# A block kernel's attention: the P-times-V bank's store in five parts, SyncE's issues in written order, stores two or three slots later

## The chip, the cores and the metric

The kernel runs on one core of one Trainium2 chip. The metric is the device time of one execution in microseconds (us); lower is better. The core has five engines that run on their own and meet through semaphores: TensorE (PE, with its weight loads shown apart as PEld), VectorE (DVE), ScalarE (ACT), GpSimd (POOL) and SyncE (SP). SP does no arithmetic here: it issues nearly all transfers between HBM and the on-chip memories. Each engine, SP too, takes its instructions strictly in the order in which the program gives them to it, and one that must wait holds up all behind it.

## The reference

A transformer block with both branches in parallel, for 2048 tokens of width 640:

```
xn  = layernorm(x)
q, k, v = split(xn @ wqkv)                       # 32 heads of 20
p   = softmax(mask(q k^T / sqrt(20)))            # a token sees itself and the 255 before it
out = x + (p v) @ wo + (gelu(xn @ w_gate) * (xn @ w_up)) @ w_down    # 1728 hidden columns
```

## The kernel before

The products in float32 are made of a high and a low part each, and three matmuls stand for one. Tokens are worked in four chunks `c` of 512, heads in eight groups `g` of four. Roughly, the program has four stages: layer norm, transposes and the first projections (to 60 to 100 us, mixed with the next); the attention, to 545 us; the gate and up products, to 804 us; and the last products with `w_down` and `wo`.

**The attention** (`attention()`, L816) is a software pipeline written out by hand. It has 32 units `u`, one for each pair of a head group and a chunk, and each unit has 14 slots (`NS`). In a slot the program first does what was put off to it (`defer(n, fn)`, L219, puts `fn` off by `n` slots; `tick()`, L807, gives out what has fallen due), then writes pieces of the attention, then fills the slot with matmuls of other work (`pull_fill`): the projections of later heads, then gate and up products. What a unit does on its slots:

- Slots 0, 5 and 9: `max_pair` (L488), score matmuls in bf16 on PE into `ps_m` (L507), and their row maxima on DVE (L517). These belong to units ahead: the pairs in slot 5 of unit u are the first of unit u+2.
- Slots 1, 3, ... 11: `exp_piece` (L558), score matmuls into `ps_e` (L572), exponentials on ACT into `P` (L574); POOL clears what the mask excludes (`clear`, L587 and L590).
- Slot 0: `av_unit(u - 1)` (L593), the P-times-V matmuls into two banks `ps_o` (L615). ACT copies both out (`ob` at L621, `oc` at L622), POOL joins them into `ob` three slots later (L625), and `store` writes `ob` to HBM five slots later (L628). `ob` has one buffer, [128, 512]: each of the four heads takes 32 of its rows, of which 20 are the output, one is the sum of the exponentials and eleven are not used.
- Slots 9 and 12: `load_stack(u + 3, ...)` (L473), the keys (slot 9) and the queries (slot 12) of unit u+3 from HBM, in six parts each (L482). There are three buffers of queries and four of keys.

**What the filler leaves to store.** A projection of queries or keys (`save_qk`, L248) is split into three bf16 parts in a tile `pt` with two buffers: ACT writes the first (`upper`, L277), DVE and ACT the second, POOL the third (`lowest`, L259), and `store` (L262) sends them to HBM in two or three transfers (L268), one slot after `lowest`. A hidden tile `he` is stored one slot after its product (L689). `x_sums` (L740) makes sums of the activations on POOL for the next stage and stores each `tx` two slots after it is made (L755). Weight tiles `wr` are loaded by `load_qk` (L232) and `load_gu` (L633).

**What sets the order on each queue.** A block `tc.manual_schedule(engines=...)` keeps the instructions of the engines it names in the order in which the program writes them. The attention's block (L871) names PE, ACT and DVE (`MANUAL`) and POOL. SP (`MANUAL_OUT`) is not among them, so the order of its issues in the attention comes from the planner of the framework, which also moves loads ahead of their place in the text. The gate-and-up stage and the last stage have blocks of their own that name SP as well.

**Where the results go.** `od[c]` is one HBM tensor per chunk, [1024, 512]: 32 rows (20 outputs, the sum, eleven unused) of each of 32 heads, row d of head h at d * 32 + h. `sd[c]` is the slice of it with the sums, which a later stage reads (L1085).

Of the kernel before, what the change touches and what calls it, by code (L numbers as in the profile page):

```python
# [9 lines left out]
F32 = mybir.dt.float32  # L10
# [7 lines left out]
S, D, H, DH = 2048, 640, 32, 20  # L18
DF = 1728
C = 512  # L20
NC = S // C
# [27 lines left out]
MANUAL_OUT = {mybir.EngineType.SP}  # L49
MANUAL = {mybir.EngineType.PE, mybir.EngineType.Activation, mybir.EngineType.DVE}  # L50
# [17 lines left out]
def block_kernel(ctx, tc, x, wqk, wv, wgu, wdo, wdl, out):  # L68
    nc = tc.nc

    const = ctx.enter_context(tc.tile_pool(name="const", bufs=1))
    dram = ctx.enter_context(tc.tile_pool(name="dram", bufs=1, space=DRAM))
# [13 lines left out]

    qd = [dram.tile([NG, 3, 4 * DH, C], BF, name=f"qd{c}") for c in range(NC)]
    kd = [dram.tile([NG, 3, 4 * DH, C], BF, name=f"kd{c}") for c in range(NC)]
    od = [dram.tile([32 * H, C], F32, name=f"od{c}") for c in range(NC)]
    sd = [t[D:D + H] for t in od]  # L90
    td = [{i: dram.tile([128, 2, C], F32, name=f"td{p}{i}") for i in (1, 2, 3, 4)} for p in range(NC // 2)]
    wtd = [dram.tile([128, 4, HD], F32, name=f"wtd{q}") if q not in OWN else None for q in range(NQD)]
    rd = [dram.tile([H, C], F32, name=f"rd{c}") for c in range(NC)]
# [1 line left out]
    hd = [hdp[f // 2][:, f % 2] for f in range(NF - 1)] + [dram.tile([NC, 64, C], F32, name="hde")]  # L95
# [102 lines left out]
    now = [None]  # L198
# [20 lines left out]
    def defer(n, fn, *a):  # L219
        if now[0] is None:  # L220
            fn(*a)
        else:
            at(now[0] + n, fn, *a)
# [24 lines left out]
    def save_qk(t, c, ps):  # L248
        pt = qkp.tile([128, 3, C], BF, name="pt", tag="pt")
        r = qkp.tile([128, C], F32, name="r", tag="r", bufs=1)  # L250
        dst = (qd if t < 5 else kd)[c]
        h, l = (2, 0) if t < 5 else (0, 2)

        def lower():
            nc.scalar.activation(pt[:, 1, :], r, AF.Copy)  # L255
            behind(lowest)

        def lowest():
            nc.gpsimd.tensor_tensor(out=pt[:, l, :], in0=r, in1=pt[:, 1, :], op=OP.subtract)  # L259
            defer(1, store)  # L260

        def store():  # L262
            a, end = t % 5 * 128, t % 5 * 128 + 128
            while a < end:
                g, b = divmod(a, 4 * DH)
                n = min(4 * DH - b, end - a)
                p = n - end + a + 128
                nc.sync.dma_start(dst[g, :, b:b + n, :].rearrange("p m t -> m p t"), pt[p - n:p])  # L268
                a += n
            done.add((t, c))  # L270

        def middle():
            nc.vector.tensor_tensor(out=r, in0=ps, in1=pt[:, h, :], op=OP.subtract)
            defer(lag(), lower)

        def upper():
            nc.scalar.activation(pt[:, h, :], ps, AF.Copy)  # L277
            late(middle)

        defer(1, upper)  # L280
# [312 lines left out]
    def av_unit(u):  # L593
        g, c = divmod(u, NC)
        v = vtiles[g]
        os = [psx.tile([128, C], F32, name="ps_o", tag="ex") for _ in range(2)]
        place = {kb - 4 * c: (pts[u, bi], col, q0) for bi, bank in enumerate(pieces(c)) for kb, col, q0, n in bank}

        def half(d, r):
            i = 2 * d + r  # L600
            return d, r, max(0, 64 * i), min(C, 64 * i + 320)

        steps_ = [((0, 0), (0, 1)), ((2, 0), (-1, 1)), ((-1, 0), (2, 1)), ((1, 0), (1, 1)),
                  ((3, 0), (-2, 1)), ((-2, 0), (3, 1))]
        todo = [half(*x) for pair in steps_ for x in pair if x[0] in place]
        begun_, left = set(), [sum(t[1] == r for t in todo) for r in range(2)]
        for d, r, qa, qb in todo:
            pt, col, q0 = place[d]
            kb = 4 * c + d
            assert (id(v), kb) in done, (u, kb)  # L610
            left[r] -= 1
            rows = slice(64 * r, 64 * r + 64)
            for j in range(4):
                w0_ = kb * 84 + 21 * j
                nc.tensor.matmul(os[r][32 * j:32 * j + 32, qa:qb], v[rows, w0_:w0_ + 32],  # L615
                                 pt[rows, j, col + qa - q0:col + qb - q0], start=r not in begun_,
                                 stop=not left[r], skip_group_check=True, tile_position=(64 * r, 32 * j))
            begun_.add(r)
        ob, oc = ap.tile([128, C], F32, name="ob", tag="ob", bufs=1), pts[u, 2][:, 0]
        lo = 0 if c else 64  # L620
        nc.scalar.activation(ob, os[0], AF.Copy)  # L621
        nc.scalar.activation(oc[:, lo:], os[1][:, lo:], AF.Copy)  # L622

        def join():
            nc.gpsimd.tensor_tensor(out=ob[:, lo:], in0=ob[:, lo:], in1=oc[:, lo:], op=OP.add)  # L625

        def store():
            nc.sync.dma_start(od[c].rearrange("(d h) t -> h d t", h=H)[4 * g:4 * g + 4], ob)  # L628

        defer(3, join)  # L630
        defer(5, store)

    def load_gu(f):  # L633
        raws = []
# [24 lines left out]
    def gate_up_fill(f, ws, c):  # L659
        cs = slice(c * C, (c + 1) * C)  # L660
        pss = []
        st = {}

        def c1():
            gs = st["g"] = hp.tile([128, C], F32, name="gs", tag="gs")
            t = st["t"] = hp.tile([128, C], F32, name="he", tag="he", bufs=2)
            nc.scalar.activation(gs, pss[0], AF.Copy, scale=0.5)
            nc.scalar.activation(t, pss[0], AF.Square, scale=math.sqrt(0.044715))
            defer(1, late, c2)

        def c2():
            gs, t = st["g"], st["t"]
            nc.vector.scalar_tensor_tensor(t, t, 1.0, gs, op0=OP.add, op1=OP.mult)
            defer(lag(), c3)

        def c3():
            nc.scalar.activation(st["t"], st["t"], AF.Tanh, scale=2.0 * math.sqrt(2.0 / math.pi))
            st["tanh"] = now[0]

        def c4():  # L680
            nc.vector.tensor_tensor(out=st["g"], in0=pss[1], in1=st["g"], op=OP.mult)
            defer(1, late, c5)

        def c5():
            if now[0] is not None and st.get("tanh", now[0]) >= now[0]:
                defer(1, late, c5)
                return
            nc.vector.scalar_tensor_tensor(st["t"], st["t"], 1.0, st["g"], op0=OP.add, op1=OP.mult)
            defer(1, lambda: nc.sync.dma_start(hd[f][c], st["t"]))  # L689

        for i, (wh, wl) in enumerate(ws):
            ps = psd.tile([128, C], F32, name="ps_d", tag="dn")
            pss.append(ps)
            yield from dense_steps(ps, lambda k: wh[:, k, :], lambda k: wl[:, k, :],
                                   lambda k: xh[:, k, cs], lambda k: xl[:, k, cs], KT)
            defer(1, *((late, c4) if i else (c1,)))
# [43 lines left out]
    def x_sums(p, k, half):  # L740
        w = C // 2
        a, b = (slice((2 * p + i) * C + half * w, (2 * p + i) * C + half * w + w) for i in (0, 1))
        eh, el = xh.bitcast(F32), xl.bitcast(F32)
        live = {}

        def tile_of(i):
            live[i] = ap.tile([128, w], F32, name="tx", tag="tx")
            return live[i]

        def pool(o, i, j, op):  # L750
            nc.gpsimd.tensor_tensor(out=o, in0=i, in1=j, op=op)  # L751

        def store(i):
            t = live[i]
            defer(2, lambda: nc.sync.dma_start(td[p][i][:, k, half * w:half * w + w], t))  # L755

        def s1():
            pool(tile_of(1), eh[:, k, b], eh[:, k, a], OP.subtract)

        def s2():  # L760
            pool(live[1], live[1], el[:, k, b], OP.add)

        def s3():
            pool(live[1], live[1], el[:, k, a], OP.subtract)
            store(1)

        def s4():
            pool(tile_of(2), eh[:, k + 2, b], live[1], OP.subtract)

        def s5():  # L770
            pool(live[2], live[2], el[:, k + 2, b], OP.add)
            store(2)

        def s6():
            pool(tile_of(4), eh[:, k + 2, a], live[2], OP.subtract)

        def s7():
            pool(live[4], live[4], el[:, k + 2, a], OP.add)
            store(4)

        def s8():
            pool(tile_of(3), eh[:, k + 2, b], eh[:, k, b], OP.subtract)

        def s9():
            pool(live[3], live[3], el[:, k + 2, b], OP.add)

        def s10():
            pool(live[3], live[3], el[:, k, b], OP.subtract)
            store(3)

        return s1, s2, s3, s4, s5, s6, s7, s8, s9, s10
# [76 lines left out]
        run(fill)  # L868
        assert not acts

    with tc.manual_schedule(engines=MANUAL | {mybir.EngineType.Pool}):  # L871
        attention()
    pr.close()
    pp.close()
# [454 lines left out]
    w = tiles, sums  # L1329
# [28 lines left out]
    for j, f in enumerate(range(NFA, NF - 1)):  # L1358
# [50 lines left out]
        if not end:  # L1409
            w = nxt_w[0], sums  # L1410
# [115 lines left out]
```

## Time and profile before

| | us |
|---|---|
| median of 3 runs (lowest, highest) | 1047.0 (1046.81, 1047.27) |
| the profiled execution's own time | 1046.35 |
| its span, first to last instruction | 1044.6 |
| PE busy / DVE / ACT / POOL | 1034.0 / 741.1 / 527.6 / 385.9 |

TensorE's granted clock is 1.00 throughout. The 16 DMA engines moved 161.60 MB, at a mean of 155 GB/s.

How to read the rows below. Times are us from the start of the span. A row of the timeline has start, duration, engine and line, operation, what is written from what is read, and how many instructions it merges; in brackets, how long the engine was idle before it and what released it. "SPq" is SP's queue issuing a transfer: the duration there is the issue alone, not the transfer. A row of the waits has who waited for whom, then total, times and longest. A row of the chain of waits has start and length of one piece of the chain that ended last; a "DMA" piece lasts from the issue until the transfer has landed. A row of the stages has the window, its length, and the busy time of PE, PEld, DVE, ACT and POOL with the number of instructions, then the clock, the share of the DMA engines' time and GB/s. Ends of matmuls are modelled, so a busy PE is not a PE at its peak.

### The profile page before, as it was taken

The page shows a single profiled execution, that of the slowest core. Times are in us where ns is not written, and L with a number is a line of the kernel's source. Part 1 is how long each engine was busy: PE and PEld are TensorE (multiplying, and loading weights), DVE is VectorE, ACT ScalarE, POOL GpSimd, SP SyncE. Part 2 cuts the span into 40 slices and gives each one's busy share as a digit, 9 for nine tenths or more (in the row PEclk, how much of TensorE's full clock was granted, in tenths as well). Part 3 has the DMA queues.
Part 4 walks back from the last instruction along what each step waited for, and adds up shares of the span by engine and source line. Part 5 has one row for each costly group of instructions (what it writes and reads, how often), then busy time and mean ns, then how long its engine had stood idle before and what let it go on. Part 6 is the DMA issues. An engine that isn't in the chain of part 4 may idle for free.

```text
span 1044.6 us, 25328 instructions
## 1 busy us (share of the span) xinstructions
PE 1034.0 (99%) x9393; PEld 834.9 (80%) x9393; DVE 741.1 (71%) x2018; ACT 527.6 (51%) x1120; POOL 385.9 (37%) x623
## 2 busy tenths in 40 slices
PE   9999999999999999999999999999999999999998
PEld 8887666666787666666678888888888999999998
DVE  7755666676656576777736788775556888888887
ACT  4534767667666666666676232223224554433332
POOL 5122778888666787667470111101110000000000
PEclk9999999999999999999999999999999999999999
DMA  5552356655533464434225575663217874433333
GB/s 211 179 162 78 115 169 175 183 170 163 160 105 107 131 177 145 139 106 154 64 85 197 177 251 206 253 244 111 78 56 254 267 248 137 137 126 121 119 121 106
DMA packets 102276, 161.60 MB, mean 155 GB/s; under 512 B 12892, under 2 KB 53980, under 8 KB 102152
## 3 DMA queue, kind: packets, MB, share of 16 engines
q1 hardware_dynamic: 99768, 153.82, 45.9%
q10 hardware_dynamic: 2384, 6.16, 1.7%
q8 instruction: 74, 1.21, 0.5%
q14 instruction: 50, 0.41, 0.1%
HBM read 101.78 MB, written 57.80 MB: 153 GB/s over the span
## 4 chain that ended last, share of the span: by engine, by line
PE 89%; DVE 4%; POOL 2%; DMA 2%; issue 1%; ACT 1%; SPq 0%; DVEq 0%; POOLq 0%; ACTq 0%
PE ps_g L970 23%; PE ps L1242 23%; PE ps_d L108 18%; PE ps_e L572 7%; PE ps_v L108 7%; PE ps_o L615 5%; PE ps_m L507 4%; DVE junk L517 2%; PE ps_g L108 1%; DMA od<-ob 1%; PE ps_d L356 1%; POOL tx L751 0%; PE ps_t L185 0%; DMA qs<-qd 0%; ACT P L574 0%
## 5 line engine op out<-in xcount | busy, mean ns | idle before, releaser
L517 DVE CUSTOM_DVE_ANT_0 junk<-ps_m,mask 128x320 bf16<-128x320 f32 (+2 forms) x512 | 242.5, 474 | 130.5 <-PE ps_m L507 72.7
L574 ACT ACTIVATE P<-ps_e 128x512 f32<-128x512 f32 (+2 forms) x384 | 198.6, 571 | 68.5 <-PE ps_e L572 67.8
L1242 PE MATMUL ps<-wb,at 128*128 128x320 f32 x999 | 155.9, 309 | 0.0
L1242 PEld LDWEIGHTS ps<-wb,at 128*128 128x128 f32 x999 | 148.9, 188 | 0.2
L587 POOL TENSOR_SCALAR_AFFINE_SELECT P<-P 128x256 f32<-128x256 f32 (+1 forms) x192 | 95.2, 498 | 72.5 <-ACT P L574 69.0
L572 PE MATMUL ps_e<-qs,ks 124*128 124x128 bf16 (+2 forms) x704 | 118.6, 278 | 0.5 <-ACT P L574 0.3
L108 PE MATMUL ps_d<-xh,wqh 128*128 128x512 f32 x310 | 99.0, 422 | 0.2 <-ACT xh L193 0.2
L108 PE MATMUL ps_d<-xl,wqh 128*128 128x512 f32 x310 | 98.5, 421 | 0.0
L108 PE MATMUL ps_d<-xh,wql 128*128 128x512 f32 x310 | 97.6, 418 | 0.0
L101 POOL TENSOR_TENSOR wql<-wr,wqh 128x640 fp32r<-128x640 f32 x12 | 19.2, 1607 | 195.4 <-PE ps_g L970 150.8
L572 PEld LDWEIGHTS <-ks 124*128 124x128 bf16 x704 | 49.5, 98 | 49.8 <-issue 35.6
L1242 PE MATMUL ps<-wt,at 128*128 128x320 f32 x552 | 88.9, 309 | 0.0
L1242 PEld LDWEIGHTS ps<-wt,at 128*128 128x128 f32 x552 | 82.9, 188 | 0.1
L590 POOL TENSOR_SCALAR_AFFINE_SELECT P<-P 128x512 f32<-128x512 f32 (+1 forms) x144 | 76.9, 542 | 16.3 <-ACT P L574 16.3
L1196 ACT ACTIVATE at<-ss 128x512 fp32r<-128x512 f32 x59 | 37.2, 631 | 82.4 <-DVE ss L1075 82.4
L615 PE MATMUL ps_o<-P,v 64*32 64x320 f32 (+4 forms) x2816 | 74.2, 347 | 0.0
L259 POOL TENSOR_TENSOR pt<-r,pt 128x512 bf16<-128x512 f32 x40 | 46.8, 1171 | 67.4 <-ACT pt L255 67.4
L507 PE MATMUL ps_m<-ks,qs 60*64 60x320 bf16 (+3 forms) x1472 | 65.4, 260 | 4.0 <-DVE mx L517 1.5
L615 PEld LDWEIGHTS ps_o<-P,v 64*32 64x32 f32 x2816 | 50.8, 106 | 21.5 <-issue 0.9
L507 PEld LDWEIGHTS <-qs 60*64 60x64 bf16 x1472 | 29.5, 105 | 44.5 <-issue 37.7
L108 PEld LDWEIGHTS ps_d<-xh,wqh 128*128 128x128 f32 x310 | 56.0, 189 | 10.5 <-issue 1.6
L108 PEld LDWEIGHTS ps_d<-xh,wql 128*128 128x128 f32 x310 | 56.0, 189 | 10.2 <-issue 1.1
(195 smaller groups left out, 1966.6 us busy)
## 6 DMA issues: line engine op xcount, KB each, us to landing
hd<-he SPq DMA_DIRECT2D x50, 256.0 KB
hr<-hd SPq DMA_DIRECT2D x48, 256.0 KB
wr<-wgu SPq DMA_DIRECT2D x27, 320.0 KB
od<-ob SPq DMA_DIRECT2D x32, 256.0 KB
qs<-qd SPq DMA_DIRECT2D x64, 120.0 KB
ks<-kd SPq DMA_DIRECT2D x64, 120.0 KB
xi<-x SPq DMA_DIRECT2D x16, 320.0 KB
qs<-qd SPq DMA_DIRECT2D x64, 80.0 KB
```

Source lines behind the costliest of these rows:

```text
L108: nc.tensor.matmul(ps, a(k), b(k), start=n == 0, stop=n == 3 * nk - 1)
L259: nc.gpsimd.tensor_tensor(out=pt[:, l, :], in0=r, in1=pt[:, 1, :], op=OP.subtract)
L507: nc.tensor.matmul(ps[64 * h:64 * h + 64, col:col + w], q[rows, j, q0:q0 + 64], ks_, start=True, stop=True, tile_position=(64 * r, 64 * h))
L517: nc.vector.tensor_tensor_reduce(out=junk[:, 0:n], in0=ps[:, 320 - n:320], in1=mask[:, 320 - n:320], scale=1.0, scalar=NEG, op0=OP.add, op ...
L572: nc.tensor.matmul(ps[:, col:col + n], k[0:QROWS, j, kc:kc + 128], q[0:QROWS, j, q0:q0 + n], start=True, stop=True)
L574: nc.scalar.activation(pt[:, j, lo:hi], ps[:, lo:hi], AF.Exp, scale=SCALE)
L587: nc.gpsimd.affine_select(out=a, in_=a, pattern=[[0, n], [1, 128]], compare_op=OP.is_ge, fill=0.0, base=0, channel_multiplier=-1)
L590: nc.gpsimd.affine_select(out=a, in_=a, pattern=[[0, n], [-1, 128]], compare_op=OP.is_ge, fill=0.0, base=-1, channel_multiplier=1)
L615: nc.tensor.matmul(os[r][32 * j:32 * j + 32, qa:qb], v[rows, w0_:w0_ + 32], pt[rows, j, col + qa - q0:col + qb - q0], start=r not in begun ...
L970: nc.tensor.matmul(ps, i, j, start=first and n == 0, stop=n == len(work) - 1, skip_group_check=True)
L1196: nc.scalar.activation(hi[:, 3:7], s, AF.Copy)
L1242: nc.tensor.matmul(ps[bank][:, 0:HD], *work[bank][j], start=bank not in begun, stop=final[p, bank] == n and j == len(work[bank]) - 1, skip ...
```

## The change

Three things. The P-times-V bank is stored without its unused rows, in five transfers: one for each head's 20 rows and one for the four rows of sums; `od[c]` becomes [640, 512] and `sd[c]` a tensor of its own, [32, 512]. SP is named in the attention's block, so it issues in the order in which the program writes. And the stores are put off for longer: that of `ob` from five slots to six, those of `pt` (from slot 1 of the attention on) and `he` from one to three, those of `tx` from two to four.

```diff
-    od = [dram.tile([32 * H, C], F32, name=f"od{c}") for c in range(NC)]
-    sd = [t[D:D + H] for t in od]
+    od = [dram.tile([D, C], F32, name=f"od{c}") for c in range(NC)]
+    sd = [dram.tile([H, C], F32, name=f"sd{c}") for c in range(NC)]
...
         def lowest():
             nc.gpsimd.tensor_tensor(out=pt[:, l, :], in0=r, in1=pt[:, 1, :], op=OP.subtract)
-            defer(1, store)
+            defer(3 if now[0] and now[0] > 0 else 1, store)
...
         def store():
-            nc.sync.dma_start(od[c].rearrange("(d h) t -> h d t", h=H)[4 * g:4 * g + 4], ob)
+            for j in range(4):
+                nc.sync.dma_start(od[c].rearrange("(d h) t -> h d t", h=H)[4 * g + j], ob[32 * j:32 * j + DH, :])
+            nc.sync.dma_start(sd[c][4 * g:4 * g + 4, :], ob[DH::32, :])

         defer(3, join)
-        defer(5, store)
+        defer(6, store)
...
-            defer(1, lambda: nc.sync.dma_start(hd[f][c], st["t"]))
+            defer(3, lambda: nc.sync.dma_start(hd[f][c], st["t"]))
...
-            defer(2, lambda: nc.sync.dma_start(td[p][i][:, k, half * w:half * w + w], t))
+            defer(4, lambda: nc.sync.dma_start(td[p][i][:, k, half * w:half * w + w], t))
...
-    with tc.manual_schedule(engines=MANUAL | {mybir.EngineType.Pool}):
+    with tc.manual_schedule(engines=MANUAL | MANUAL_OUT | {mybir.EngineType.Pool}):
         attention()
```

## The prediction

> **What bounds the kernel now.** I read the busy times by stage first, then what TensorE (PE) waited for, then the chain of waits around one of those stalls, then SyncE's (SP's) queue there, issue by issue.
>
> ```profile
> PE 1034.0 (99%) x9393; PEld 834.9 (80%) x9393; DVE 741.1 (71%) x2018; ACT 527.6 (51%) x1120; POOL 385.9 (37%) x623
> ```
> ```profile
> 105.00:280.00 175.00, 173.03 (x2278) 114.90 (x2277) 118.25 (x439) 119.25 (x246) 144.55 (x242) 1.00 0.56 163
> ...
> 350.00:545.00 195.00, 193.45 (x2521) 128.35 (x2522) 129.04 (x455) 130.60 (x262) 136.52 (x234) 1.00 0.41 124
> 545.00:804.00 259.00, 259.00 (x1180) 214.52 (x1171) 179.00 (x296) 85.40 (x157) 29.41 (x20) 1.00 0.51 179
> ```
>
> The second fence has window, length, then busy time of PE, its weight loads, DVE, ACT and POOL. PE is busy 99% of the span at clock 1.00. The change acts on the attention, 105 to 545 us. In the two stretches shown of it PE idles 1.97 + 1.55 = 3.52 us, and from 545 to 804 not at all. Work saved on SP or in transfers is worth only what it takes out of those 3.52 us; a new wait has no such limit.
>
> ```profile
> PE ps_m L507 <- DVE mx L517: 1.1, 4, 0.4
> PE ps_m L507 <- DMA qs<-qd: 0.9, 3, 0.5
> PE ps_e L572 <- ACT P L574: 0.3, 1, 0.3
> PE ps_m L507 <- DVE r L273: 0.2, 1, 0.2
> ```
> ```profile
> 151.53 0.29 PE L507 MATMUL ps_m<-ks,qs 60*64 60x256 bf16 x1
> 152.38 0.47 PE L507 MATMUL ps_m<-ks,qs 60*64 60x256 bf16 x15 [0.55 <-DMA qs<-qd]
> ...
> 196.09 0.47 PE L507 MATMUL ps_m<-ks,qs 60*64 60x256 bf16 x15 [0.21 <-DVE r L273]
> ```
>
> What PE waited for (total, times, longest; 105 to 545 us), and its largest stall: the second matmul of a unit's first max pair waits for the end of that unit's query load. The 0.2 us put down to DVE r stands before the same matmul of another unit, so I count it with them.
>
> ```profile
> 137.27 1.24 POOL ob L625
> ...
> 138.53 7.20 DMA od<-ob
> 145.75 2.92 DMA ks<-kd
> ```
> ```profile
> 138.53 0.52 SPq L628 DMA_DIRECT2D od<-ob  x1
> 139.10 0.47 SPq L234 DMA_DIRECT2D wr<-wqk  x1
> 139.67 6.39 SPq L482 DMA_DIRECT2D ks<-kd  x6
> 146.60 1.03 SPq L482 DMA_DIRECT2D qs<-qd  x3
> 147.74 2.11 SPq L268 DMA_DIRECT2D qd<-pt  x3
> 149.96 1.06 SPq L482 DMA_DIRECT2D qs<-qd  x3
> ```
> ```profile
> SPq L482 <- DMA od<-ob: 16.3, 8, 3.4
> SPq L268 <- DMA od<-ob: 10.4, 3, 3.9
> SPq L268 <- POOL pt L259: 9.6, 9, 1.6
> SPq L628 <- POOL ob L625: 9.1, 7, 4.8
> ```
>
> The chain, SP's queue and SP's waits (105 to 280 us) tell why the load is late. The store of the joined bank leaves at 138.53 and lands 7.20 us later. The sixth part of the key load behind it shares no data with it, yet goes out only at 145.75, on its landing: an issue waits for a transfer some seven places ahead. So the queries leave between 146.60 and 151.02, as PE comes to need them. Such waits cost SP 16.3 + 10.4 = 26.7 us in these twelve units (175 us at 14.48, the distance of two P-times-V below).
>
> **The change, part by part.**
>
> *Five parts for one store.* It removes 32 stores of 256 KB and adds 128 of 40 KB (20 rows) and 32 of 8 KB. An undisturbed load of six parts in SP's queue, and two landings from the chain:
>
> ```profile
> 491.60 2.24 SPq L482 DMA_DIRECT2D ks<-kd  x6
> ```
> ```profile
> 250.69 2.30 DMA qs<-qd
> ...
> 265.29 2.46 DMA qs<-qd
> ```
>
> One issue of a six-part load takes 2.24/6 = 0.37 us, so five take 1.87 against the 0.52 of the store at 138.53: 1.35 us more per unit, 43 us over 32 units, all on SP. A 40 KB store of 20 rows is not in the trace. Bounds for its landing are 2.30 us (a query load's part) and 7.20 us (the present store); I take 2.46, since a third of the parts of a stack load have just 20 rows and 40 KB. The last part then lands about 4.0 us after the first issue (1.50 + 2.46), and the issue seven places behind finds the first one done. So 26.7 us of SP's waits go, for 12 x 1.35 = 16 us of added issue in the same stretch. The Trainium skill speaks on both sides, in "DMA: Bandwidth & Descriptors". Its section "Why a DMA increments its semaphore by 16 and not by 1" says a transfer is spread over as many engines, up to 16, as divide the outermost sizes of both sides: 4 for the old store (a destination of 4 heads), 10 for 20 rows. The 7.20 us agree, and by it my 2.46 us stands. Its "Rules for kernel authors" want small transfers coalesced, since under 64 KB one pays mostly overhead; by it the five would cost more than the one, which is rival D.
>
> *SP in written order, with later stores.* I walk it through the unit that begins with this P-times-V:
>
> ```profile
> 130.84 2.45 PE L615 MATMUL ps_o<-P,v 64*32 64x320 f32 x96
> ...
> 145.32 2.45 PE L615 MATMUL ps_o<-P,v 64*32 64x320 f32 x96
> ```
> ```profile
> 141.62 1.16 POOL L259 TENSOR_TENSOR pt<-r,pt 128x512 bf16<-128x512 f32 x1 [1.36 <-ACT pt L255]
> ```
> ```profile
> 133.01 1.44 SPq L268 DMA_DIRECT2D qd<-pt  x3
> ```
>
> The written order is: the pt store of the tile before (slot 2), td (slot 5), the five parts (6), the key load (9), the next pt store (11), the query load (12). The parts wait for POOL's join, which ends at 138.51, and hold back everything after them. Parts to 140.4; six key parts to 142.6; POOL's pt is ready at 142.78, its three issues end at 144.2; six query parts, at the key load's pace, end at 146.5; the last lands near 148.6, 2.9 us before PE's need at 151.53. Now it is issued at 150.6 or so and lands near 153. The stalls by query loads (0.9 + 0.2 us) go, and the 0.3 us for ACT, which stands a unit's end behind a late pt store. Sum: 1.4 us. Bounds: 3.52 us, if every idle moment of the two stretches goes; below nothing, the price of rival D. I take the value by the stalls named.
>
> *Later pt store and its two buffers.* ACT's L277 overwrites a pt buffer two tiles later, about a unit on, and waits for its store:
>
> ```profile
> ACT pt L277 <- DMA qd<-pt: 0.5, 1, 0.5
> ```
>
> Two slots are near 2 us (14.48 us for 14 slots). But the store that the code writes earlier now leaves at 147.74, 5 us after POOL was done at 142.78; in the new order it leaves at once. I cost it at 0; what covers it is this delay going away. Uncovered, 2 us of late ACT could reach the exponentials once a tile, which rival D holds in its price.
>
> *td and he two slots later, od and sd as two tensors, 88 KB less per store.* Tile tx and tile he have two buffers each, reused a unit or more later. The sums are first read long after the last store:
>
> ```profile
> 548.22 0.53 SPq L628 DMA_DIRECT2D od<-ob  x1
> ...
> 559.22 0.61 PE L970 MATMUL ps_g<-xh,wqh 128*128 128x512 f32 x2
> ...
> 576.99 0.93 SPq L1085 DMA_DIRECT2D rc<-od  x2
> ```
>
> 28.8 us cover 1.3 us more of issue. ACT and POOL wait for five transfers before ob is overwritten, not one, but ACT stands 58.3 us in all before that copy waiting for PE:
>
> ```profile
> ACT ob L621 <- PE ps_o L615: 58.3, 26, 3.5
> ```
>
> All of these at 0; without cover, some tenths of a us.
>
> The sum against the profiled execution: 1046.35 us (span 1044.6 and 1.75 around it) - 1.4 = 1044.95. The runs' median, 1047.0, is 0.65 above it, so **1045.6 us**. Where does the stall go? PE is the next bound everywhere, so what PE gains stays gained.
>
> **The rivals.**
>
> A, the forecast: 1045.6, own range 1044.9 to 1046.5.
>
> B, nothing reaches PE: the loads come in time but DVE's max reductions, 1.1 us of PE's idle now, end the same moments a little later. For it: DVE's is the largest of PE's waits. Against it: the stall at 152.38 has a transfer as its releaser. 1046.9.
>
> C, all idle goes, also that of DVE and ACT, which are served by POOL and by buffers freed earlier. For it: POOL is 83% busy from 105 to 280 (144.55/175). Against it: 1.55 us of the idle lies after 350, where few stores block SP. 1047.0 - 3.5 = 1043.5.
>
> D, slower: the parts do not land sooner and the added issue falls on the query load. Place: SP, between POOL's join and slot 12. For it: SP is in strict order, and POOL's join ended up to 4.8 us after SP stood ready for it. Against it: the 2.9 us of reserve above, and six-part loads that land 2.5 us after issue. It decides once SP falls back more than those 2.9 us; then each of the 12 units from 105 to 280 can pay up to 1.35 us (16 us), and the four that stall already pay it surely (5.4 us). Between them 11: 1058.
>
> E, slower: written order loses loads that are now sent ahead of the text.
>
> ```profile
> 43.99 2.42 SPq L482 DMA_DIRECT2D qs<-qd  x6
> ...
> 60.61 0.80 SPq L268 DMA_DIRECT2D kd<-pt  x2
> ```
> ```profile
> 58.83 0.26 PE L507 MATMUL ps_m<-ks,qs 60*64 60x64 bf16 x6
> 59.29 0.66 PE L185 MATMUL ps_t<-ident,xi 128*128 128x128 f32 x4 [0.20 <-DVE xl L194]
> ```
>
> If the first stack went behind the store at 60.61, its queries and keys (twice 2.42 us of issue) would have landed at 61.4 + 4.8 + 2.9 = 69.1, 10.3 us after PE's first use. At the end, weight loads held behind the last parts (548.22 + 1.87 = 550.1) would still have 9 us, against a landing of 2.92, before the matmul at 559.22. Against it: at 58.83 PE, in written order within the attention, already works for it ahead of the last transposes of the stage before, so stages mix though orders are fixed. Between 0 and 10.3, I take 4, since the end costs nothing: 1051.
>
> **How the numbers follow.** A 48%, B 17%, C 12%, D 13%, E 10%. A measurement of this kernel can tell about 0.2%, 2.1 us, from no change. Faster by more: C and the edge of A, 15%. Slower: D and nearly all of E, 22%. Within: 63%. The range must hold A, B and nearly all of C, and half of E: 1043.6 to 1050.5, leaving out D and the rest of E. Cases of both signs are in it; the likeliest one's own is 1044.9 to 1046.5.
>
> **What would show it.** Right: SP's waits for od gone from L482 and L268; no PE wait for qs; the query load of each unit issued as one run of six; PE's idle from 105 to 280 down from 1.97 to about 0.6. D: PE waits for qs in many units, and SP's time between the parts and the queries longer than 6 us. E: a PE gap near 59 or 559. B: PE's waits for qs gone with the idle unchanged. I am wrong if the parts land as late as the old store, or if POOL's join comes more than 3 us later against PE than now.

## The result, and the profile after

| | before | after | ratio (95% interval) |
|---|---|---|---|
| median of 11 runs each (lowest, highest), us | 1047.0 (1045.64, 1048.86) | 1044.12 (1043.59, 1046.42) | 0.9973 (0.9965 to 0.9982) |
| profiled execution, us | 1046.35 | 1045.72 | |
| its span, us | 1044.6 | 1044.0 | |

The change makes the kernel faster by 0.27%, 2.9 us. The profiled execution of after is one of its longer ones; a second set of runs, profiled in an execution of 1043.73 us, is among the experiments (`after_again`) and is used here beside the first. In that second set the gain was smaller: 0.11%, 1.5 us.

The same views as before, first the waits of SP (105 to 280 us) and SP's queue in the unit that the prediction walked through:

```profile
SPq L629 <- POOL ob L625: 20.3, 8, 4.8
SPq L268 <- POOL pt L259: 11.0, 11, 2.3
SPq L482 <- DMA qs<-mr: 5.6, 3, 2.5
```
```profile
138.53 1.42 SPq L629 DMA_DIRECT2D od<-ob  x4
140.00 0.51 SPq L630 DMA_DIRECT2D sd<-ob  x1
140.60 2.55 SPq L482 DMA_DIRECT2D ks<-kd  x6
143.59 1.31 SPq L268 DMA_DIRECT2D qd<-pt  x3
145.00 2.26 SPq L482 DMA_DIRECT2D qs<-qd  x6
```

No wait for `od` is left, where there were 26.7 us. The six key parts go out in one run of 2.55 us (6.39 before, held by the old store), and so do the six query parts, from 145.00 to 147.26; before, the last of them was issued at about 151. What SP waits for now is POOL: it stands ready before the join is done.

Then the stages, with window, length and the busy time of PE, weight loads, DVE, ACT and POOL, and what PE waited for from 105 to 545:

```profile
105.00:280.00 175.00, 173.96 (x2306) 116.12 (x2306) 119.02 (x443) 120.82 (x252) 145.26 (x243) 1.00 0.55 162
350.00:545.00 195.00, 193.44 (x2536) 128.69 (x2537) 129.85 (x454) 130.78 (x263) 136.78 (x234) 1.00 0.38 119
```
```profile
PE ps_m L507 <- DVE mx L517: 1.1, 4, 0.4
PE ps_m L507 <- DMA qs<-qd: 0.6, 1, 0.6
```

Idle from 105 to 280 falls from 1.97 to 1.04 us, and after 350 stays as it was (1.55 and 1.56). One stall by a query load is left, a new one. But the reader should not stop at the idle. The first P-times-V, the first gate-and-up product and the first matmul of the last stage mark the stages' limits; rows of the timeline of before, of after and of `after_again`:

```profile
102.10 1.93 PE L615 MATMUL ps_o<-P,v 64*32 64x320 f32 x64
...
545.49 1.43 PE L108 MATMUL ps_g<-xh,wqh 128*128 128x512 f32 x5
...
804.05 2.21 PE L1242 MATMUL ps<-wb,at 128*128 128x320 f32 x14
```
```profile
102.09 1.93 PE L615 MATMUL ps_o<-P,v 64*32 64x320 f32 x64
...
543.38 1.43 PE L108 MATMUL ps_g<-xh,wqh 128*128 128x512 f32 x5
...
802.11 4.12 PE L1244 MATMUL ps<-wb,at 128*128 128x320 f32 x27
```
```profile
101.94 1.93 PE L615 MATMUL ps_o<-P,v 64*32 64x320 f32 x64
...
542.27 1.42 PE L108 MATMUL ps_g<-xh,wqh 128*128 128x512 f32 x5
...
801.00 5.29 PE L1244 MATMUL ps<-wb,at 128*128 128x320 f32 x35
```

From the first to the second mark, the attention takes 443.39 us before, 441.29 after and 440.33 in the second profile: 2.10 and 3.06 us less, where the idle from 105 to 280 fell by only 0.93 and 1.54 us. Gate and up take 258.6 to 258.7 in all three. The rest of the difference between the spans is in the last stage.

**A stall costs more than the idle shown.** The largest stall of before (151.53 and 152.38 in the prediction) is gone in the second profile, and a new one of the same kind stands in the first:

```profile
151.26 0.47 PE L507 MATMUL ps_m<-ks,qs 60*64 60x256 bf16 x16
```
```profile
165.64 0.27 PE L507 MATMUL ps_m<-ks,qs 60*64 60x256 bf16 x1
166.48 0.47 PE L507 MATMUL ps_m<-ks,qs 60*64 60x256 bf16 x15 [0.57 <-DMA qs<-qd]
```

Undisturbed, the sixteen matmuls of a max pair take 0.47 us together. They are short, use a part of the array each and start some 0.01 us behind one another, while each is listed with 0.19 to 0.29 us. When the second waits for its load, the row shows only the idle after the first one's end: 0.55 us at 152.38, where the starts are 0.85 apart; 0.57 at 166.48, where they are 0.84 apart. All these profiles hold the same 9393 matmuls in the same order, so each matmul can be laid beside its twin in another profile. Beside the second profile of after, the four stalls that the prediction counted (152.38, 196.09, 253.12, 267.88) were worth 0.84 + 0.50 + 0.44 + 0.52 = 2.30 us, and showed as 1.15.

**The last stage.** In the first profile of after, PE stops there once:

```profile
835.99 2.29 PE L1244 MATMUL ps<-wb,at 128*128 128x320 f32 x14 [0.81 <-DVE xr L1267]
```
```profile
793.37 7.27 DMA stg<-wdo
```

The second fence is a piece of the chain of waits that ends in this stall: a load of `w_down` that takes 7.27 us to land, after which ACT's and DVE's splitting of the weights runs late until DVE's first additions of the output do. The second profile has no such stall. From its first matmul to the span's end the stage takes 240.6 us before (1044.6 - 804.05), 241.9 after, and 240.9 in the second profile. (The recorded texts below count it to PE's last matmul: 237.2, 238.6 and 237.6.) Here too the stall costs more than its 0.81 us of idle: PE's lead over the kernel before falls from 1.94 to 0.84 us between 830 and 840.

### The profile page after: what moved, and what is told of

The parts are those of the page before. It is cut to its first block, busy times and chain, and to the rows that moved or that the text cites. A ratio compares the mean times of both kernels' runs of the same rounds, so it can differ in the third digit from the quotient of the medians.

```text
span 1044.0 us, 25563 instructions
## 1 busy us (share of the span) xinstructions
PE 1033.4 (99%) x9393; PEld 834.3 (80%) x9393; DVE 741.7 (71%) x2018; ACT 527.5 (51%) x1120; POOL 385.5 (37%) x623
## 4 chain that ended last, share of the span: by engine, by line
PE 90%; DVE 5%; ACT 2%; DMA 2%; issue 1%; POOL 0%; ACTq 0%; DVEq 0%; SPq 0%
PE ps_g L972 22%; PE ps_d L108 20%; PE ps L1244 20%; PE ps_e L572 8%; PE ps_v L108 7%; PE ps_o L615 5%; PE ps_m L507 5%; DVE junk L517 2%; PE ps_g L108 1%; DMA stg<-wdo 1%; ACT wb L1058 1%; PE ps_d L356 1%; PE ps_t L185 0%; DVE wb L1077 0%; DMA qs<-qd 0%
```

## The experiments

All were timed beside runs of the kernel before on the same chip, whose medians were 1047.01 (29 runs), 1047.05 (16) and 1047.05 (13) for the three groups of four below; the third group ran on another chip than the first two. "Attention" is the distance from the first P-times-V to the first gate-and-up product in the profile, against 443.39 before. In the recorded texts, `ps_g` is that first gate-and-up product, at 545.49 us before.

| run | parts | SP's order | stores | od, sd | median (range, runs) | ratio (95%) | attention |
|---|---|---|---|---|---|---|---|
| `five_alone` | five | planner | as before | new | 1046.6 (1043.95 to 1048.4, 12) | 0.999 (0.998 to 1.0) | -2.04 |
| `written_alone` | one | written | as before | old | 1048.19 (1046.6 to 1050.15, 11) | 1.0011 (1.0002 to 1.0019) | +1.84 |
| `written_late` | one | written | later | old | 1053.16 (1051.24 to 1054.06, 5) | 1.0052 (1.004 to 1.0064) | +6.30 |
| `five_written` | five | written | as before | new | 1048.05 (1046.46 to 1051.54, 12) | 1.0008 (0.9995 to 1.0021) | +0.09 |
| `after_again` | five | written | later | new | 1045.58 (1043.46 to 1049.65, 12) | 0.9989 (0.9978 to 0.9999) | -3.06 |
| `after_keep` | five | written | later | old | 1043.72 (1043.48 to 1045.2, 5) | 0.9965 (0.9953 to 0.9977) | -2.82 |
| `whole` | one, rows together | planner | as before | own | 1043.48 (1043.03 to 1044.11, 5) | 0.996 (0.9947 to 0.9973) | -3.20 |
| `whole_late` | one, rows together | written | later | own | 1043.47 (1043.1 to 1043.87, 5) | 0.9961 (0.9948 to 0.9973) | -3.11 |
| `five_keep` | five | planner | as before | old | 1044.97 (1044.51 to 1045.65, 7) | 0.9976 (0.9965 to 0.9986) | -1.67 |
| `five_late_keep` | five | planner | later | old | 1043.77 (1043.52 to 1044.05, 6) | 0.9963 (0.9951 to 0.9974) | -3.03 |
| `pt_late_keep` | five | written | pt later | old | 1044.44 (1043.68 to 1044.66, 5) | 0.9966 (0.9954 to 0.9978) | -2.23 |
| `after_pad` | five | written | later | new, padded | 1044.01 (1043.7 to 1044.65, 5) | 0.9965 (0.9953 to 0.9977) | -2.90 |

### One part of the change at a time

`five_alone` has the hunks of `od`, `sd` and `store`, with `defer(5, store)`.

> The store in five parts alone; the planner's order on SP and the old delays. Theory L (the landing): what cost PE was the 7.2 us of the old store, on which SP stood; with it gone the units from 145 to 275 us lose most of their stretch: the first gate-and-up matmul, at 545.49 before and 543.38 after, comes at 543.4 to 544.2, time 0.1 to 0.2% below before. Rival O (the order): the planner's order, which splits the query loads and puts pt stores between them, is what makes them late; then it stays at 545 to 545.5 and the time within 0.05% of before. SP's waits for od in L482 and L268 go in either case.

The gate-and-up products begin at 543.52 us, as theory L had it: the attention is 2.04 us shorter, nearly the 2.10 of the first profile of after. The waits of its SP (105 to 280 us) have no `od` in them either:

```profile
SPq L629 <- POOL ob L625: 16.3, 10, 4.8
SPq L268 <- POOL pt L259: 12.1, 12, 1.7
SPq L757 <- POOL tx L753: 4.4, 8, 0.8
```

Yet the median gains only 0.4 us, and the runs spread over 4.5 us. The profiled one (1047.35 us) loses it in the last stage, at the same place as after:

```profile
837.71 1.55 PE L1244 MATMUL ps<-wb,at 128*128 128x320 f32 x9 [2.44 <-DVE xr L1267]
```

`written_alone`:

```diff
-    with tc.manual_schedule(engines=MANUAL | {mybir.EngineType.Pool}):
+    with tc.manual_schedule(engines=MANUAL | MANUAL_OUT | {mybir.EngineType.Pool}):
```

> SP named in the attention's block, nothing else: one store, old delays. Theory O: the gate-and-up stage begins at 543.4 to 544.2. Theory L: the old store still blocks the key and query loads behind it, in written order as before; it begins at 545 to 546.5, and stores one slot after their producer hold SP longer on POOL (waits of L268 and L628 up), so the time is at or above before.

The written order by itself costs 1.2 us at the median, and the gate-and-up products begin at 547.48 us, later than either theory gave. SP stands at a pt store for POOL (from 105 to 280; 9.6 us before) with loads behind it that the planner had put ahead.

```profile
SPq L268 <- POOL pt L259: 25.2, 11, 3.5
```

This is the likely reason, but such waits do not cost PE anything by themselves: `whole_late`, further down, has 25.0 us of them in the written order and no stall by a query load.

`written_late` adds the four later delays, still with the one old store.

> Written order and the later stores, with the one store of 256 KB. Theory L: the store's 7.2 us still stand between the parts of the key load; the stage begins at 544.6 to 546, waits of SP for od stay above 15 us. Theory O: 543.4 to 544.2, as with everything.

```profile
PE ps_m L507 <- DMA qs<-qd: 6.6, 9, 1.6
```
```profile
SPq L268 <- POOL pt L259: 14.3, 10, 3.0
...
SPq L268 <- DMA od<-ob: 9.7, 3, 4.5
SPq L482 <- DMA od<-ob: 7.4, 3, 2.9
...
SPq L234 <- DMA od<-ob: 3.5, 1, 3.5
```

The worst of all, 6.1 us above before, with the gate-and-up products at 552.16 us, which neither theory gave. SP waits less for POOL, but the old store stands a slot later, and 20.6 us (9.7 + 7.4 + 3.5) of waits for its landing now fall on the pt store and the loads behind it. PE waits nine times for its queries, in six units. Not all of the loss is waiting, though:

```profile
170.02:173.43 3.41, 3.41 (x26) 2.19 (x18) 2.00 (x8) 1.74 (x4) 2.35 (x4) 0.50 0.52 135
```

For these 3.41 us, right after two of the stalls (1.60 and 0.82 us of idle), TensorE's granted clock is 0.50. Laid beside the second profile of after, PE falls another 1.55 us behind there, so 4.75 of the 6.30 us are left for the waits. (The one run of this set at a mean clock of 1.00 took 1051.24 us.) Whether the stalls brought the lower clock, no run shows. Beside the one old store, in written order, the late stores do harm; beside stores that land soon they do not.

`five_written` has the five parts and the written order, with the old delays.

> Five parts and written order with the old delays: tells what the later stores add. Both theories: SP waits longer for POOL at pt and ob stores, which now stand ahead of the key load by up to two slots. If the later stores matter, the stage begins 0.5 us or more after 543.4; if they are only a precaution, at 543.2 to 543.8.

The attention is as long as before, and the products begin at 545.77 us, so by that text the later stores matter. The parts gave back what the written order had cost, no more; PE still waits four times for queries:

```profile
PE ps_m L507 <- DMA qs<-qd: 2.2, 4, 0.8
```
```profile
140.17 0.50 SPq L630 DMA_DIRECT2D sd<-ob  x1
142.84 1.33 SPq L268 DMA_DIRECT2D qd<-pt  x3
144.28 2.75 SPq L482 DMA_DIRECT2D ks<-kd  x6
147.13 2.77 SPq L482 DMA_DIRECT2D qs<-qd  x6
```

With the old delay the pt store stands ahead of the keys: SP waits for POOL until 142.84, the keys leave at 144.28 instead of 140.60 as in the change, and the queries at 147.13 instead of 145.00.

### The landing apart from the parts

`whole` and `whole_late` keep one store of 256 KB, but let a group's 128 rows lie together in HBM, in a tensor `oh` beside `od`. The order of rows is put right where the quotients are made:

```diff
+    oh = [dram.tile([32 * H, C], F32, name=f"oh{c}") for c in range(NC)]
+    sd = [t.rearrange("(h d) t -> d h t", d=32)[DH] for t in oh]
...
-            nc.sync.dma_start(od[c].rearrange("(d h) t -> h d t", h=H)[4 * g:4 * g + 4], ob)
+            nc.sync.dma_start(oh[c][128 * g:128 * g + 128], ob)
...
-                nc.sync.dma_start(t, rows)
+                raw = oh[i].rearrange("(h k q) t -> q h k t", k=8, q=4)
+                for q in range(4):
+                    nc.sync.dma_start(t[32 * q:32 * q + 32], raw[q, :, self.ks[0]:self.ks[-1] + 1])
```

> One store of 256 KB as before, in the planner's order with the old delays, but into a tensor whose 128 rows of a head group lie together (row 32 * head + d), so that source and destination agree row by row; the jobs of the gate-and-up stage that divide by the sums read it from there in four parts and write the quotient, in the old order of rows, to another tensor. Theory L (what hurt was that the store lands 7.2 us after its issue): the store lands in about 2.5 to 3.5 us, SP's waits for od go, and the attention ends as with the five parts alone, ps_g at 543.5 us or sooner, since SP issues one transfer and not five; median 1044.5 to 1046. Theory F (the gain came from having fewer bytes or more, smaller transfers): as before, ps_g at 545.5, median 1047.

> The same one store into rows that lie together, with SP in written order and the later stores of the change. Theory L: as the changed kernel or better, ps_g at 543.4 us or up to 1 us sooner (1.35 us less of SP's issue in each unit), no PE wait for qs of more than 0.6 us; median 1043 to 1045. Theory F: as the run with one old store, written order and later stores, ps_g at 552, median 1053.

The same bytes as before (161.60 MB) and the same number of stores, and the attention is 3.20 us shorter. By the trace's record of each transfer's end, the 32 stores land 2.04 us after their issue in the median (1.96 to 3.92), the old ones 6.52 (5.39 to 8.64) and the 40 KB parts of the change 1.53. So neither the number of transfers nor the bytes, but the landing held SP. It held more than the waits put down to `od`: in the kernel before, the weight load behind the store (139.10) and the first five key parts (139.67 to 142.28) landed 5.9 to 7.4 us after their issue, while the key parts of the same unit in after took 2.0 to 2.8. SP's next issues (146.60, 146.97, 147.30) left within 0.1 us of such landings (146.54, 146.96, 147.22). This is what the Trainium skill, "DMA: Bandwidth & Descriptors", section "Rules for kernel authors", would have advised: the outermost size of both sides sets how many engines take a transfer, so the 128 partitions should stand outermost. The runs agree, 2.04 us against 6.52 for the same 256 KB, and the trace has 5 completion records (updates of a transfer's semaphore) for each old store, 11 for each 20-row part and 16 for each wide store. That the rows lie together in HBM is not what it takes: in `after_keep` the 20-row parts go to the same scattered rows as the old store and land in 1.53 us. Its other rule there, to coalesce what is under 64 KB, is no rival to it: the one wide store beats the five narrow ones too (1043.48 against 1044.97 in `five_keep`). It costs SP one issue instead of five; that this is the reason is not shown.

SP's queue in `whole` in the same unit, then the stages:

```profile
138.49 0.34 SPq L629 DMA_DIRECT2D oh<-ob  x1
138.88 0.42 SPq L235 DMA_DIRECT2D wr<-wqk  x1
139.40 2.36 SPq L483 DMA_DIRECT2D ks<-kd  x6
144.30 1.02 SPq L483 DMA_DIRECT2D qs<-qd  x3
```
```profile
105.00:280.00 175.00, 174.57 (x2314) 117.01 (x2314) 120.19 (x446) 121.28 (x254) 145.91 (x245) 1.00 0.56 168
```

The store is also quicker to issue, 0.34 us against 0.52. Idle from 105 to 280 is 0.43 us, and what PE still waits for is DVE's maxima (1.0 us from 105 to 545). The written order and the later stores add nothing to it: `whole_late` is 0.01 us from it. `whole` beats both kernels: all five of its runs lie under the lowest run of before, and its median is 0.64 us under that of the first set of after and 2.1 under that of the second, which ran beside it. Over after this is mostly the spread of the runs: the attention of `whole` is only 0.13 us shorter than that of the second profile.

### The order and the delays, with parts

`five_keep`, `five_late_keep` and `pt_late_keep` write the five parts to the old tensors, as `after_keep` does:

```diff
-            nc.sync.dma_start(od[c].rearrange("(d h) t -> h d t", h=H)[4 * g:4 * g + 4], ob)
+            for j in range(4):
+                nc.sync.dma_start(od[c].rearrange("(d h) t -> h d t", h=H)[4 * g + j, 0:DH], ob[32 * j:32 * j + DH, :])
+            nc.sync.dma_start(sd[c][4 * g:4 * g + 4, :], ob[DH::32, :])
```

> The five parts alone (the planner's order, the old delays), written into the old tensors: od [1024, 512], the sums a slice of it. Theory T (the smaller od and the separate sd move the tensors in HBM, and with that some executions lose 1 to 4 us to later landings): median 1043.5 to 1044.5 with a narrow spread, where the five parts alone with the new tensors had 1046.6 (1043.95 to 1048.4); last stage 237.2 us. Theory W (those 2.6 us are the price of the planner's order or of the old delays): median 1046 to 1047 again, spread as wide. In both, the attention ends 2 to 3.2 us sooner than before, ps_g at 542.3 to 543.5.

> As the run before it, with the later stores added, still in the planner's order. Theory L (the landing is all that matters and the planner puts loads ahead of waiting stores anyway): the same time within 0.5 us, ps_g within 0.5 us. A rival: the later stores have a worth of their own in any order, then 0.5 to 2 us less than the run before it; or they come too late for the loads of the next units, then 1 us or more above it.

> Five parts into the old tensors, SP in written order, and of the later stores only that of pt (three slots instead of one). Theory P (in written order the loss came from SP standing at a pt store for POOL, with the query load behind it): as the whole change in the old tensors, 1043.5 to 1044.5, ps_g 542.3 to 543.4, no PE wait for qs over 0.6 us. Theory O (the later store of ob matters, or that of td and he): 1046 to 1048 as the five parts in written order without later stores, ps_g at 544.5 to 545.8, PE waits for qs of 1 us or more.

`five_keep` lies between what the two theories gave, 1044.97, with a narrow spread and no stall in the last stage; its attention is 1.67 us shorter, less than the 2 to 3.2 that both gave. `five_late_keep` contradicts my theory: the later stores have a worth of their own in the planner's order, 1.20 us, and no run of the one is within the range of the other. The profile says where, though not why:

```profile
PE ps_m L507 <- DMA qs<-qd: 1.0, 2, 0.5
```
```profile
222.96 0.29 PE L507 MATMUL ps_m<-ks,qs 60*64 60x256 bf16 x1
223.73 0.47 PE L507 MATMUL ps_m<-ks,qs 60*64 60x256 bf16 x15 [0.48 <-DMA qs<-qd]
```

These are rows of `five_keep`; in `five_late_keep` PE waits for no query load. SP's waits for POOL's pt are 12.1 us there (105 to 280) and 8.6 with the later stores, those for tx 4.3 and 1.4. But these waits do not explain the gain: `whole` has 26.2 us of them for pt, with the old delays, and no stall. And in the unit of the first stall (152.35) the last two query parts leave at the same moments in both profiles (146.77 and 147.16; 146.80 and 147.18) and land at 152.22 and 152.46 in `five_keep`, at 151.10 and 151.34 in `five_late_keep`: there the landing was later, not the issue. How the later stores bring the 1.20 us stays open. With the stores late, the written order is worth nothing more: `after_keep` has 1043.72, `five_late_keep` 1043.77. And in written order, of the later stores that of pt is worth most, as theory P had it: `pt_late_keep` is at 1044.44 with one stall of 0.5 us left and an attention 2.23 us shorter than before, where `five_written`, without later stores, had four stalls and an attention as long as before. (Its median, 1048.05, was taken in the new tensors, which have their own loss in the last stage.) The rest, 0.7 us to `after_keep`, is in ob, td and he together; I did not part them.

### The last stage

`after_again` is the changed kernel itself; `after_keep` is the change with the old tensors; `after_pad` has the new tensors, with `sd` so large that all that is allocated behind lies where it lay:

```diff
-    sd = [dram.tile([H, C], F32, name=f"sd{c}") for c in range(NC)]
+    sd = [dram.tile([32 * H - D, C], F32, name=f"sd{c}")[0:H] for c in range(NC)]
```

> The changed kernel once more, beside the next three. Theory L (the store's landing held SP's later issues; the five parts land soon and the later delays keep SP from waiting for POOL): the gate-and-up products begin at 543.4 us again, 2.1 us sooner than before, and the median is 1044 to 1045. For the last stage: if its stall of 0.81 us belongs to the kernel and not to chance, this profile has it too (238.0 to 240 us for the stage, against 237.24 before); if it is chance from run to run, the stage may come out at 237.2.

> The changed kernel with the tensors of before: od stays [1024, 512] with the sums as a slice of it, and the five parts go to the same rows as the old store's. The unused rows of od are neither written nor read. Theory T (the last stage is longer because od and sd lie elsewhere in HBM, so that transfers of that stage meet each other): last stage 237.2 us, no stall, and the median 0.5 to 2 us under the changed kernel's. Theory V (the last stage's stall comes with the moment at which the stage starts, or by chance, and the layout has no part in it): stage and median as the changed kernel's, within 1 us. In both the attention ends as in the changed kernel, ps_g at 543.4.

> The changed kernel with sd made as large as the rows that od gave up ([384, 512], of which only the 32 rows of sums are written and read), so that all tensors behind them lie where they lay before, while od and sd themselves lie as in the change. Theory T1 (what lies behind od and sd was moved, td, hd and the staged weights, and that costs some executions 1 to 4 us): median 1043.5 to 1044.2, spread narrow. Theory T2 (od's own place decides): as the changed kernel, 1044 to 1045.6 and a spread up to 1047 or more. Theory V (chance from launch to launch, no tensor's place): also as the changed kernel, and the runs in the old tensors beside it are then as wide.

The changed kernel's second set has its median at 1045.58 and reaches from 1043.46 to 1049.65, though its profiled execution shows the best attention of this kernel and no stall: what is lost differs from execution to execution of one program. Counting the runs more than 1.2 us above the lowest of their own kernel: 26 of 47 where the tensors behind `od` and `sd` were moved by the change (2 of 11 in the first set of after, 9 of 12 in the second, 8 of 12 in `five_alone`, 7 of 12 in `five_written`); 1 of 28 in the five kernels with parts that leave them where they were. That fits the theory that the moved tensors make later landings more likely, and `after_pad`, at 1044.01 and narrow, would then say that it is those behind, not `od` itself. But four of those five kernels, `after_pad` among them, ran on another chip than `after_again`. And the kernel before, with everything in its old place, spreads as well (28 of its 58 runs beside the experiments, by the same count; 1045.6 to 1051.59 in the first 29), the two sets of one and the same kernel differ as 2 of 11 and 9 of 12, and `whole` moves the tensors behind by another amount and spreads little. Why a load lands late in some executions stays open; that the parts cannot be blamed is shown by the kernels with parts and a narrow spread.

## Why the prediction was right and wrong

**The time.** 1045.6 was forecast and 1044.12 measured; it lies in the range 1043.6 to 1050.5 and below the forecast's own range, 1044.9 to 1046.5. That it would be faster by over 0.2% had 0.15.

**The mechanism was right.** The landing of the old store held SP, and with it the query load. `whole` shows it alone: one store, the same bytes, the planner's order and the old delays, and the stalls go with the landing. What the prediction did not have is that the transfers behind the store landed late as well (5.9 to 7.4 us) and held SP in their turn. Of the signs that were named two came in both profiles: no wait for `od` on L482 or L268, and the query load as one run of six. The other two, no stall by a query load and idle of about 0.6 us from 105 to 280, came in the second profile (none, 0.43) and not in the first (one, 1.04).

**The term that was mis-sized** is the sum of 1.4 us: 0.9 + 0.2 for the query loads and 0.3 for ACT, taken from the idle of the rows of waits. The four query stalls were worth 2.30 us, not the 1.15 that the rows show, since each idle is counted from the listed end of a matmul that others overlap. With them went 0.39 us of the waits for ACT (157.65 and 158.14, 0.43 + 0.25, less 0.29 that the second profile loses itself just ahead of them) and 0.37 us in smaller steps: 3.06 us in the second profile. The rows of the prediction held it: 152.38 - 151.53 = 0.85. The same error stands in the bound "gains are worth only what they take out of the 3.52 us of idle": 0.43 us of idle is left of 1.97 in `whole`, and the attention is 3.20 us shorter.

**The walk through a unit** was right for SP (parts to 140.5, forecast 140.4; query load out by 147.3, forecast 146.5) and too hopeful about the landing. By the record of ends the last query part lands at 151.0, 4.1 us after its issue, not at 148.6. So the reserve in that unit is about 0.4 us and not 2.9, and one unit of the first profile used it up (166.48). The parts landed sooner than the 2.46 us taken, in 1.53.

**The later pt store, costed at 0**, is worth 1.2 us together with the other stores in the planner's order, and in the written order it is what makes the change pay (the attention is 2.23 us shorter than before with that of pt alone, as long as before without later stores). I asked only whether it could delay ACT, and did not ask what is queued behind a store that waits for POOL. For td, he and the two tensors no cost shows in the attention, as put, though td and he were not run alone.

**The rivals.** B fell: the idle went and more went with it. C, 1043.5, is what the kernel reaches in its best runs, though by stalls that cost more than they show and not by all idle going: the 1.56 us after 350 us stayed. D did not come in this change, since the parts land sooner; but its place was right, as `written_late` shows: once a landing falls on the query load in strict order, the price is 6 us, 1.55 of it at the halved clock. E did not come at either end: the first max pair starts within 0.02 us of where it did, and the gate-and-up products follow without a gap. That written order loses what the planner hoisted is nevertheless true within the attention, at 1.2 us (`written_alone`). What I had not on the list is the last stage, where late loads reach PE in some executions; it cost the profiled execution 1.1 us. In the second set more than half of the gain is missing (1045.58 against 1043.72 in `after_keep`); where those executions lose it is not shown, since the one that was profiled has no stall there.

## What to carry to other kernels

Price a stall by the distance of the starts, against an undisturbed twin of the same matmuls, not by the idle beside it: where matmuls overlap, the idle shows a half of it here. Where an issue queue waits for a transfer that shares no data with what it holds up, look first at how the two sides of that transfer are cut: with the 128 rows outermost on both sides the same 256 KB landed in 2.0 us instead of 6.5, and the new order, the parts and the delays were needless. And try the parts of a change in each other's company: the later stores cost 5 us beside the slow store (1048.19 to 1053.16, part of it at a halved clock), gain 1.2 us beside the five parts, and nothing beside the one wide store.

## What the runs showed of the hardware that I had not expected

The way a store is cut changes the price of its issue as well: 0.53 us in the median for the old store of 256 KB and 0.34 for the one with rows together. Five parts of 40 and 8 KB take 1.9 us of SP, yet land 1.5 us (1.7 for the 8 KB) after the issue of each, sooner than the one wide store. And one program's runs lay between 1043.46 and 1049.65. The first profile of after shows a late landing, 7.27 us for a load of `w_down` in the last stage that took 5.6 in the trace of the kernel before. The clock has a part too: in each of the seven sets of the experiments that have executions at a granted clock of 0.998 or 0.997, thirteen in all, these are the longest of their set, as the two longest of `after_again` are (1047.59 and 1049.65). One stretch like that of `written_late`, 3.41 us at half the clock, makes 0.998 of a whole execution. It is not all: the third longest of `after_again`, 1047.29, ran at 1.00.
